# Experts after a linear attention: weight parts loaded earlier, two row transposes placed later

## The chip, the cores and the metric

The kernel runs on one NeuronCore of one Trainium2 chip. The metric is device time in microseconds (us) of one execution, as the median of several runs. The profile shows one execution, with every instruction's start and duration by engine: PE (TensorE, with PEld for its weight loads), DVE (VectorE), ACT (ScalarE), POOL (GpSimd), SP (SyncE, which here only issues DMA transfers).

## The reference, cut to what matters

The change lies in the last of three stages, a mixture of eight experts in which each token goes to its two best experts. x is the stage's input of 2304 rows by 512.

```python
top2 = np.argpartition(-noisy_logits, 2, axis=1)[:, :2]
...
for e in range(E):
    for k in range(2):
        mask = top2[:, k] == e
        ...
        h = np.maximum(x[mask] @ w1[e], 0.0)
        out[mask] += top2_w[mask, k, None] * (h @ w2[e])
```

w1[e] is 512 by 1024, w2[e] is 1024 by 512. The other two stages (attention with exponential features, a wide layer with a maximum of three products) are not touched.

## The kernel before, in words

Every float32 product is made of three matmuls, since each operand is split into a rounded high part and the remainder: high by high, high by low, low by high. So each weight part is held as a pair `wh`, `wl`, and each activation as a pair too (`gx`, and `hh`, `hl` for the hidden layer).

**Units.** The experts' work is a list of units, numbered n. Unit 0 is expert 0 with 512 rows, unit 1 is expert 0 again with 128 rows, and units 2 to 8 are experts 1 to 7 with 608 rows each (row tiles 0 to 4: four of 128 rows and one of 96). In units 2 to 8 the first product is done in a scheme with seven block products instead of eight (`product`, L1213): in two rounds of two column blocks f, each round goes through the seven products in the order 1, 6, 7, 4, 5, 3, 2. Their sums are formed by DVE (`sum7`, L1232, tiles `u`, `v`, `t`), ACT takes the maximum with zero and makes `hh` (L1241, L1242), and POOL or DVE makes `hl` (L1251, L1249). A product's PSUM bank is free for a later product when ACT or DVE has read it. The banks are three named `s`, three named `p` and `k`, and two named `t`, each used in turn. Then `expert2` (L1354) multiplies the hidden layer by w2: 24 matmuls for each row tile, into a `p` or `k` bank. In the second round the two banks of product 4 are `t` banks, and the first two transposes of the next unit's rows use them next.

**Rows of the next unit.** POOL gathers the token rows of the next unit by indirect DMA (`gather_x`, L1139) into one of two buffers (`gx`, `xg` in the trace). PE transposes a row tile in four small matmuls (`turn_x`, L1149; `turns7` in the plan). Then ACT and DVE split the transposed rows and form block sums (`x_quarters`, `x_sums`; `rows7(j)` for a pair of row tiles). Row tile i + 2 is gathered into the buffer that row tile i leaves. Results go out by a gather of the old rows (`pv`), a DVE multiply-add (`o`, L1362) and a scatter (`out_dram`, L1364), all in POOL's queue.

**Weight parts.** A part of 128 by 1024 comes in three steps: a 512 KB transfer into one of two `raw` buffers, issued by SP (L1381 for w2, L1387 for w1); the copy to `wh` on ACT (L1434); the remainder `wl` on DVE (L1442). So the transfer of part n + 2 waits for the `wl` of part n. The sums of w1 blocks that products 6, 7, 5 and 3 need were made ahead of time and come ready split from memory (`wh<-sums`, `wl<-sums`, L1437), each waiting until PE has done with the part whose place it takes.

**Order.** All instructions of PE, ACT, DVE and SP are written out by a plan: each step is given a time on a rough clock (`clock[0]`, advanced by `pe` with the length of a PE step), and the steps are sorted by it. The times set only the order in each engine's queue. Queues run strictly in order, so a waiting instruction holds up those behind it. POOL's indirect transfers keep the order of the plan too. `refill_at(i, t, lead)` puts the transfer of part i at t - lead, its `wh` at t and its `wl` at t + 1.2, counted from the clock at which it is called.

For the refill behind unit 1, six parts are loaded. This text calls them A to F in the order of their transfers: A is the w1 part for product 2 of unit 2; B, C, D and E are the four w2 parts of unit 2, in the order in which `expert2` uses them; F is the w1 part for product 1 of unit 3. They are x = 0, 1, 3, 4, 2, 5 in the code. Behind them come G and H, the w1 parts for products 4 and 2 of unit 3.

Of the kernel before, what the change touches and what calls it, by code (L numbers as in the profile page):

```python
# [38 lines left out]
def tile_linear_attention__then__moe__then__noisy_top2_moe(  # L39
# [29 lines left out]
    F2 = FF2 // P  # L69
# [53 lines left out]
    def bank_acc():  # L123
        turns["acc"] += 1
        return bank_k() if turns["acc"] % 3 == 0 else bank_p()
# [973 lines left out]
    def sizes(M):  # L1099
        return [min(P, M - i * P) for i in range((M + P - 1) // P)]  # L1100
# [96 lines left out]
    def seven(n):  # L1197
        return isinstance(n, int) and n > SEVEN
# [139 lines left out]
    def expert2(n, e, M, i, fs=tuple(range(F2))):  # L1338
        m = sizes(M)[i]
        cs = slice(i * P, i * P + m)  # L1340
        p_ = st.pop(("eo", n, i)) if fs[0] else bank_acc()[:m]
        if seven(n):
            fs = (0, 1, 4, 5, 6, 7, 2, 3)
        for f in fs:
            wh, wl = WE[e, (len(ORDER7) if seven(n) else KD) + f // 2]
            hh, hl = st["eh", n, f]
            fw = slice((f % 2) * DM, (f % 2) * DM + DM)
            if seven(n):
                ps_ = slice((i // 2) * 2 * P + i % 2, (i // 2 + 1) * 2 * P, 2)
                hh, hl = (h[:, ps_] if i < 4 else h[:, cs] for h in (hh, hl))  # L1350
            else:
                hh, hl = (h[:, cs] for h in (hh, hl))
            for r, (a, b_) in enumerate(((hh, wh), (hh, wl), (hl, wh))):
                nc.tensor.matmul(p_, a, b_[:, fw], start=(f == 0 and r == 0),  # L1354
                                 stop=(f == (3 if seven(n) else F2 - 1) and r == 2))
        st["eo", n, i] = p_
# [182 lines left out]
    def pe(dur, f, *x):  # L1539
        at(clock[0], f, *x)  # L1540
        clock[0] += dur
# [44 lines left out]
    for i, n in enumerate(late_ones[1:]):  # L1586
        t = END + (3.2 + 2.6 * i + 3.0 * (i > 5) if i else 0.2)
# [143 lines left out]
    for n, (e, M, row0) in enumerate(units):  # L1731
        n_now[0] = n
        nsp = 1 if M <= 512 else 2
        cw = M // nsp
        nxt = n + 1 < len(units)
        if nxt:
            e2, M2, row2 = units[n + 1]
            nt2 = len(sizes(M2))
        g0 = clock[0]
        d1 = 3 * KD * cw / 2400  # L1740
        if seven(n):
            for two in ((0, 1), (2, 3)):
                for q_ in ORDER7:
                    for f in two:
                        pe(2 * 3 * HN / 2400, product, n, e, q_, f)
                        d0, d = (-0.03, 0.01) if two[0] and q_ == ORDER7[-1] else (0.02, 0.44)
                        after(d0, sum7, n, q_, f)
                        if q_ in PART7:
                            after(d0 + d, relu7, n, q_, f)
                            after(d0 + 2 * d, low7, n, q_, f)  # L1750
                    if two[0]:
                        room(base(e) + ORDER7.index(q_))
        elif M > P:
            for f in range(F2):
                for s in range(nsp):
                    if n == 0:
                        for i in range(2):
                            pe(d1 / 2, expert1, n, e, M, f, s, cw, range(2 * i, 2 * i + 2))
                            if f < 2:
                                tail(NCHUNK - 1, 2 * f + i)  # L1760
                    else:
                        pe(d1, expert1, n, e, M, f, s, cw)
                    after(0.0, expert_hidden, n, f, s, cw)
                if n == 0 and f == 1:
                    after(0.0, open_experts)
                    tp = clock[0] + 0.01
        else:
            pe(2.56, tile1, n, e, 0)
            after(0.0, tile_relu, n, 0)
            pe(1.28, tile1, n, e, 1, range(2))  # L1770
            pe(0.45, tile_turn, n, 0)
            after(0.0, tile_hidden, n, 0)
            pe(1.28, tile1, n, e, 1, range(2, KD))
            after(0.0, tile_relu, n, 1)
            after(0.01, gather_prev, 1, 0, cap_b, 0)
        if seven(n):

            own = [i for i in range(base(e), base(e) + len(ORDER7))
                   if i < len(pairs) and not summed(*pairs[i])]
            for i, t in zip(own, (7.0, 9.5, 16.5)):  # L1780
                refill_at(i, t, 9.0)
        elif n:
            rooms(base(e), 2)
            for i in range(2):
                after(0.3 + 0.6 * i, w2_high, *pairs[base(e) + i])
        if n == 4:
            st["table"] = overflow_table()
        if n in (4, 5):
            for i in range(9 - (n == 5)):
                at(g0 + 2.0 + 2.3 * i, next, st["table"])  # L1790

        if n > 1:
            tp = g0 + 12.0
        if n != 1:
            for i in range(min(3, len(sizes(M)))):
                at(tp, gather_prev, n, e, M, i)
        if n == 0:
            for n_ in (1, 2):
                _, M_, row_ = units[n_]
                at(tp + 17.0, load_meta, n_, row_, M_, 0)  # L1800
            at(tp + 17.1, gather_x, 1, cap_b, 0, N + 1)
            at(tp + 20.0, gather_x, 2, cap, 0, N + 1)
        elif n > 1 and nxt:
            for i in range(2):
                at(g0 - 3.0, gather_x, n + 1, M2, i, N + 1)
        if 0 < n and n + 2 < len(units):
            at(g0 + (6.2 if n == 1 else 2.3), load_meta, n + 2, units[n + 2][2], cap, 0)
        d2 = 3 * F2 * DM / 2400
        def turns7(i, n=n):
            pe(0.45, turn_x, n + 1, cap, i)  # L1810
            if i + 2 < len(sizes(cap)):
                after(0.02, gather_x, n + 1, cap, i + 2, N + 1)

        def rows7(j, wait=1.6):
            after(0.5, x_quarters, j)
            after(wait, x_sums, j)

        if M <= P:
            pe(0.7 * 2, expert2, n, e, M, 0, range(2))
            pe(0.45, tile_turn, n, 1)  # L1820
            after(0.0, tile_hidden, n, 1)
            turns7(4)
            rows7(2)
            pe(0.7 * 2, expert2, n, e, M, 0, range(2, 4))
            pe(d2 / 2, expert2, n, e, M, 0, range(4, F2))
            after(0.0, expert_out, n, e, M, 0)
        else:
            if nxt and n > 0:
                for i in range(2):
                    turns7(i)  # L1830
                rows7(0)
            if not nxt:
                after(0.9, settle)
            for i in range(len(sizes(M))):
                if n == 0 and i == 2:
                    pe(0.45, turn_x, 1, cap_b, 0)
                    after(0.02, gather_x, 2, cap, 1, N + 1)
                    turns7(0, 1)
                if n == 0 and i == 3:
                    turns7(1, 1)  # L1840
                    rows7(0)
                pe(d2, expert2, n, e, M, i)
                if n == 0:
                    after((-0.01, -0.01, 0.5, 0.5)[i], expert_out, n, e, M, i)
                else:
                    after(0.95 if nxt and i == 1 else -0.01, expert_out, n, e, M, i)
                if n == 0 and i == 2:
                    after(0.51, gather_prev, n, e, M, 3)
                elif n and i + 3 < len(sizes(M)):
                    after(0.96 if nxt and i == 1 else 0.0, gather_prev, n, e, M, i + 3)  # L1850
                if nxt and n > 1:
                    if i == 1:
                        turns7(2)
                        turns7(3)
                        rows7(1)
                    if i == 3:
                        turns7(4)
                        rows7(2)
        if n == 0:
            turns7(2, 1)  # L1860
            turns7(3, 1)
            rows7(1, 2.6)
        if n:
            if seven(n):
                i = base(e) + len(ORDER7)
                rooms(i, 4)
                for x, t in enumerate((0.4, 3.8, 12.7, 15.8)):
                    refill_at(i + x, t, 9.0)
            else:
                i = base(e) + 2  # L1870
                rooms(i, 6)
                for x, t in zip((0, 1, 3, 4, 2, 5), (0.4, 3.4, 6.2, 12.7, 15.8, 18.6)):
                    refill_at(i + x, t, 4.0 if x == 5 else 9.0)

    ET = mybir.EngineType
# [56 lines left out]
```

## Time and profile before

| what | value |
|---|---|
| median of 3 runs | 935.04 us (933.77 to 935.37) |
| profiled execution | 935.69 us |
| its span from first to last instruction | 934.1 us |
| outside the span | 1.6 us |
| PE busy | 924.6 us, 99% of the span |
| DVE, POOL, ACT busy | 616.9, 540.7, 491.6 us |
| granted PE clock | 0.998 of full speed (2.4 GHz) |
| moved by DMA | 178.07 MB, mean 191 GB/s |

The PE is busy nearly all the time. Durations of matmuls overlap (they are pipelined), so progress of PE is read from the distance between starts. A wait is read in the bracket behind an instruction: the idle time before it, and what ended it.

### The profile page before, as it was taken

To read this page: it belongs to the slowest core of one execution; us is meant where nothing else is said; L and a number is where in the kernel's file an instruction comes from. 1 tells how busy PE (TensorE), PEld (TensorE's weight loads), DVE (VectorE), ACT (ScalarE), POOL (GpSimd) and SP (SyncE) were. 2 spreads that over 40 slices of the span, in tenths; PEclk is the share of its full clock that TensorE was granted. 3 is DMA by queue.
4 is the path that set the end of the run, shared out by engine and by line. 5 is a ranking of instruction groups with operands and counts; after the bars stand their busy time and mean duration, and the time that the engine had idled before them with its cause. 6 is when DMAs were issued, how large, how long until landed. Compare 5 with 4: busy or idle time off the path is not lost. (4 is left out here: it accounts for less than half of the span.)

```text
span 934.1 us, 18533 instructions
## 1 busy us (share of the span) xinstructions
PE 924.6 (99%) x6817; PEld 805.1 (86%) x6817; DVE 616.9 (66%) x1292; ACT 491.6 (53%) x1056; POOL 540.7 (58%) x598
## 2 busy tenths in 40 slices
PE   9999999999999999999999999999999999999997
PEld 7677777799999999999997889798898989898895
DVE  6999999997563737364564367667576767567641
ACT  7999999554333334343445147355463635455340
POOL 6788898645554645646443546465574746455362
PEclk9999999999999999999999999999999999999999
DMA  7676663544757575857575367666575856748212
GB/s 195 171 220 170 185 192 104 193 154 138 227 178 251 181 239 178 248 170 216 164 218 204 91 224 248 242 215 233 174 254 175 285 166 204 264 155 296 94 34 73
DMA packets 131101, 178.07 MB, mean 191 GB/s; under 512 B 35998, under 2 KB 90398, under 8 KB 131010
## 3 DMA queue, kind: packets, MB, share of 16 engines
q1 hardware_dynamic: 119522, 146.94, 49.5%
q0 software_dynamic: 10928, 29.62, 9.5%
q8 instruction: 54, 0.88, 0.4%
q10 hardware_dynamic: 560, 0.33, 0.1%
q14 instruction: 37, 0.30, 0.1%
HBM read 123.05 MB, written 51.24 MB: 187 GB/s over the span
## 5 line engine op out<-in xcount | busy, mean ns | idle before, releaser
L899 PE MATMUL s<-xh,wh 128*128 128x384 f32 x432 | 147.3, 341 | 0.0
L899 PE MATMUL s<-xh,wl 128*128 128x384 f32 x432 | 145.2, 336 | 0.0
L899 PE MATMUL s<-xl,wh 128*128 128x384 f32 x432 | 145.1, 336 | 0.0
L1364 POOL DMA_INDIRECT out_dram<-o,emeta x40 | 47.7, 1191 | 97.6 <-DVE o L1362 30.1
L909 DVE TENSOR_TENSOR a<-s,a 128x384 f32<-128x384 f32 x72 | 40.0, 555 | 88.4 <-PE s L899 87.3
L899 PEld LDWEIGHTS s<-xh,wh 128*128 128x128 f32 x432 | 81.1, 188 | 5.4 <-DVE a L909 2.5
L1354 PE MATMUL p<-wh,hh 128*128 128x512 f32 (+1 forms) x208 | 82.9, 399 | 0.0
L1354 PE MATMUL p<-wh,hl 128*128 128x512 f32 (+1 forms) x208 | 82.5, 396 | 0.2 <-POOL hl L1251 0.2
L899 PEld LDWEIGHTS s<-xl,wh 128*128 128x128 f32 x432 | 81.1, 188 | 1.4
L1354 PE MATMUL p<-wl,hh 128*128 128x512 f32 (+1 forms) x208 | 82.1, 395 | 0.0
L899 PEld LDWEIGHTS s<-xh,wl 128*128 128x128 f32 x432 | 81.1, 188 | 0.0
L1442 DVE TENSOR_TENSOR wl<-raw,wh 128x1024 fp32r<-128x1024 f32 x57 | 69.3, 1221 | 14.8 <-ACT wh L1434 13.8
L1213 PE MATMUL s<-gx,wh 128*128 128x304 f32 x336 | 72.5, 302 | 0.0
L1410 POOL TENSOR_TENSOR raw<-raw 128x256 f32<-128x256 f32 x28 | 24.5, 876 | 74.9 <-DMA raw<-in_moe_w_dram 63.4
L132 DVE TENSOR_TENSOR gx<-t,gx 128x512 fp32r<-128x512 f32 (+3 forms) x88 | 41.0, 480 | 35.7 <-ACT gx L131 32.8
L1434 ACT ACTIVATE wh<-raw 128x1024 fp32r<-128x1024 f32 x57 | 58.9, 1053 | 9.4 <-DMA raw<-in_moe_w_dram 9.4
L245 POOL TENSOR_TENSOR nm<-nm,bits 128x512 int32<-128x512 int32 (+1 forms) x32 | 38.2, 1205 | 40.9 <-DVE nm L235 16.1
L916 ACT ACTIVATE hh<-a 128x384 fp32r<-128x384 f32 x36 | 18.8, 523 | 81.1 <-DVE a L909 76.9
L131 ACT ACTIVATE gx<-t 128x512 fp32r<-128x512 f32 (+3 forms) x88 | 36.5, 437 | 39.3 <-DVE t L1188 30.5
L1213 PEld LDWEIGHTS s<-gx,wh 128*128 128x128 f32 x336 | 55.6, 189 | 0.7
L1077 POOL DMA_INDIRECT meta<-mt,si x36 | 38.8, 1077 | 29.7 <-DVE si L1073 20.5
L1213 PE MATMUL s<-gx,wl 128*128 128x304 f32 x168 | 50.9, 303 | 0.0
(323 smaller groups left out, 2635.0 us busy)
## 6 DMA issues: line engine op xcount, KB each, us to landing
raw<-in_moe_w_dram SPq DMA_DIRECT2D x57, 512.0 KB
raw<-in_moe_w_dram SPq DMA_DIRECT2D x56, 256.0 KB
sums<-qh SPq DMA_DIRECT2D x28, 512.0 KB
sums<-raw SPq DMA_DIRECT2D x28, 512.0 KB
wh<-sums SPq DMA_DIRECT2D x28, 512.0 KB
wl<-sums SPq DMA_DIRECT2D x28, 512.0 KB
bits<-in_moe_w_dram SPq DMA_DIRECT2D x18, 512.0 KB
out_dram<-zrow SPq DMA_DIRECT2D x9, 512.0 KB
```

The costliest lines, as they stand in the source:

```text
L131: nc.scalar.activation(hi, src, AF.Copy)
L132: nc.vector.tensor_tensor(lo, src, hi.bitcast(F32), op=ALU.subtract)
L245: in_order(nc.gpsimd.tensor_tensor(m_[:, i:i + w], m_[:, i:i + w], low[:, i:i + w], op=ALU.add))
L899: nc.tensor.matmul(p_, a[:, d, fs], b_, start=(n == 0), stop=(n == 3 * KD - 1))
L909: nc.vector.tensor_tensor(a, p_, st.pop("a"), op=ALU.max)
L1077: ins = nc.gpsimd.indirect_dma_start(out=meta, out_offset=bass.IndirectOffsetOnAxis(ap=si[:, t, kk:kk + 1], axis=0), in_=mt[:, t, kk, :], ...
L1213: nc.tensor.matmul(bk["p"], a[:, d, fs], b_[:, d, :], start=(d == 0 and i == 0), stop=(d == 1 and i == 2))
L1354: nc.tensor.matmul(p_, a, b_[:, fw], start=(f == 0 and r == 0), stop=(f == (3 if seven(n) else F2 - 1) and r == 2))
L1364: alone(e, nc.gpsimd.indirect_dma_start(out=out, out_offset=bass.IndirectOffsetOnAxis(ap=mt[:m, i, 1:2], axis=0), in_=o[:m], in_offset=Non ...
L1410: ins = nc.gpsimd.tensor_tensor(a22, a21, a22, op=ALU.add)
L1434: nc.scalar.activation(WE[e, i][0], st["w2", e, i], AF.Copy)
L1442: nc.vector.tensor_tensor(wl, st.pop(("w2", e, i)), wh.bitcast(F32), op=ALU.subtract)
```

## The change

In the refill behind unit 1, the times of the `wh` copies of A to F were 0.4, 3.4, 6.2, 12.7, 15.8 and 18.6 us on the plan's clock, and are now 0.4, 1.8, 4.8, 7.6, 10.4 and 13.2. Their transfers, which are placed 9 us ahead (4 for F), move with them. In unit 2 only, the transposes of row tiles 2 and 3 of unit 3 stood behind row tile 1 of `expert2`; they stand now in the middle of row tile 2, between its matmuls for four column blocks and for the other four. For this `expert2` takes a range of blocks, and translates it to its own order of blocks.

```diff
         if seven(n):
-            fs = (0, 1, 4, 5, 6, 7, 2, 3)
+            fs = [(0, 1, 4, 5, 6, 7, 2, 3)[f] for f in fs]
...
-                pe(d2, expert2, n, e, M, i)
+                if n == 2 and i == 2:
+                    pe(d2 / 2, expert2, n, e, M, i, range(4))
+                    turns7(2)
+                    turns7(3)
+                    rows7(1)
+                    pe(d2 / 2, expert2, n, e, M, i, range(4, F2))
+                else:
+                    pe(d2, expert2, n, e, M, i)
...
-                    if i == 1:
+                    if i == 1 and n > 2:
                         turns7(2)
...
-                for x, t in zip((0, 1, 3, 4, 2, 5), (0.4, 3.4, 6.2, 12.7, 15.8, 18.6)):
+                for x, t in zip((0, 1, 3, 4, 2, 5), (0.4, 1.8, 4.8, 7.6, 10.4, 13.2)):
                     refill_at(i + x, t, 4.0 if x == 5 else 9.0)
```

What this does to the queues is shown at three places. The first is SP's queue from part A on. Before, the row with x3 ends with A, the next L1381 is B, the x3 behind it are C, D and E, and the lone L1387 is F:

```order
L1387 DMA raw<-in_moe_w_dram 128x2x512 x3
L1437 DMA wh<-sums 128x1024
L1437 DMA wl<-sums 128x1024
L1381 DMA raw<-in_moe_w_dram 128x2x512
L1437 DMA wh<-sums 128x1024
L1437 DMA wl<-sums 128x1024
L1381 DMA raw<-in_moe_w_dram 128x2x512 x3
L1437 DMA wh<-sums 128x1024
L1437 DMA wl<-sums 128x1024
L1387 DMA raw<-in_moe_w_dram 128x2x512
```

The same place in the changed kernel:

```order
L1387 DMA raw<-in_moe_w_dram 128x2x512 x3
L1381 DMA raw<-in_moe_w_dram 128x2x512
L1437 DMA wh<-sums 128x1024
L1437 DMA wl<-sums 128x1024
L1437 DMA wh<-sums 128x1024
L1437 DMA wl<-sums 128x1024
L1381 DMA raw<-in_moe_w_dram 128x2x512 x3
L1387 DMA raw<-in_moe_w_dram 128x2x512
L1437 DMA wh<-sums 128x1024
L1437 DMA wl<-sums 128x1024
```

B stands now ahead of the two sums for unit 2, and F ahead of the first sum for unit 3. The three other sums for unit 3, and G and H behind them, keep their places.

The second place is DVE's queue at the start of unit 2's seven products. Before (the L1442 rows are the `wl` of A, B and C; `u`, `v`, `t` are the sums of the first round):

```order
L1442 TENSOR_TENSOR wl<-raw,wh 128x1024
L1232 TENSOR_TENSOR u<-s_7245,t 128x304
L1232 TENSOR_TENSOR u<-k,t 128x304
L1232 TENSOR_TENSOR v<-s_7269,u 128x304
L1232 TENSOR_TENSOR v<-p_7279,u 128x304
L1442 TENSOR_TENSOR wl<-raw,wh 128x1024
L1232 TENSOR_TENSOR t_7288<-t_7288,v 128x304
L1232 TENSOR_TENSOR t_7300<-t_7300,v 128x304
L1249 SCALAR_TENSOR_TENSOR hl_7223<-t_7288,hh_7222 128x304
L1232 TENSOR_TENSOR v<-s_7309,v 128x304
L1232 TENSOR_TENSOR u<-s_7309,u 128x304
L1249 SCALAR_TENSOR_TENSOR hl_7235<-t_7300,hh_7234 128x304
```

And in the changed kernel:

```order
L1442 TENSOR_TENSOR wl<-raw,wh 128x1024
L1232 TENSOR_TENSOR u<-s_7245,t 128x304
L1442 TENSOR_TENSOR wl<-raw,wh 128x1024
L1232 TENSOR_TENSOR u<-k,t 128x304
L1232 TENSOR_TENSOR v<-s_7273,u 128x304
L1232 TENSOR_TENSOR v<-p_7282,u 128x304
L1232 TENSOR_TENSOR t_7291<-t_7291,v 128x304
L1442 TENSOR_TENSOR wl<-raw,wh 128x1024
L1232 TENSOR_TENSOR t_7301<-t_7301,v 128x304
L1249 SCALAR_TENSOR_TENSOR hl_7223<-t_7291,hh_7222 128x304
L1232 TENSOR_TENSOR v<-s_7313,v 128x304
L1232 TENSOR_TENSOR u<-s_7313,u 128x304
```

The `wl` of B moved ahead of three sums, and that of C ahead of three sums and two `hl`. Further on, D, E and F move the same way: D stands behind the first of product 3's two sums, E directly ahead of the second round's first sum, F behind that round's two `u`. ACT's `wh` copies move with them: C's follows B's directly, D's stands behind the first `v` pair of round one, E's ahead of the last `t` pair of round one, and F's behind the two copies of product 1 of round two.

The third place is PE's queue between row tiles 1 and 2 of unit 2 (`t` rows are the transposes, `k` is the bank of row tile 1, `p` that of row tile 2). Before:

```order
L1354 MATMUL k<-wh,hl_7396 128x512
L1149 MATMUL t_7673<-exact,gx 128x128 x4
L1149 MATMUL t_7678<-exact,xg 128x128 x4
L1354 MATMUL p_7684<-wh,hh_7220 128x512
L1354 MATMUL p_7684<-wl,hh_7220 128x512
```

And in the changed kernel, twelve matmuls of row tile 2 further on:

```order
L1354 MATMUL p_7673<-wl,hh_7234 128x512
L1354 MATMUL p_7673<-wh,hl_7235 128x512
L1149 MATMUL t_7694<-exact,gx 128x128 x4
L1149 MATMUL t_7699<-exact,xg 128x128 x4
L1354 MATMUL p_7673<-wh,hh_7387 128x512
```

In POOL's queue one row moves with them: the gather of row tile 4 goes from ahead of the scatter of row tile 1 to behind the `pv` gather of row tile 4. No instruction is added or taken away on any engine.

## Rows read from the trace of the kernel before

**Rows 1.** The page, part 1: busy us, share of the span, instructions.

```profile
PE 924.6 (99%) x6817; PEld 805.1 (86%) x6817; DVE 616.9 (66%) x1292; ACT 491.6 (53%) x1056; POOL 540.7 (58%) x598
```

**Rows 2.** The waits of PE in the whole span: us in total, times, longest.

```profile
PE t L1149 <- DMA gx<-x2d,emeta: 0.9, 1, 0.9
...
PE p L1354 <- POOL hl L1251: 0.2, 1, 0.2
```

**Rows 3.** The timeline of PE in unit 2, around its two waits.

```profile
583.41 0.39 PE L1354 MATMUL p<-wl,hh 128*128 128x512 f32 x1
583.95 0.51 PE L1354 MATMUL p<-wh,hl 128*128 128x512 f32 x1 [0.16 <-POOL hl L1251]
...
590.25 0.40 PE L1354 MATMUL k<-wl,hh 128*128 128x512 f32 x1
590.48 0.40 PE L1354 MATMUL k<-wh,hl 128*128 128x512 f32 x1
591.76 0.50 PE L1149 MATMUL t<-exact,gx 128*128 128x128 f32 x4 [0.89 <-DMA gx<-x2d,emeta]
...
592.76 0.48 PE L1354 MATMUL p<-wh,hh 128*128 128x512 f32 x1
```

**Rows 4.** The timeline of PE at the same pair of transposes without a wait, between units 0 and 1.

```profile
541.40 0.39 PE L1354 MATMUL p<-wh,hl 128*128 128x512 f32 x1
...
542.27 0.46 PE L1286 MATMUL s<-wh,x 128*128 128x512 f32 x1
```

**Rows 5.** The timeline of SP: transfers of C to E, of F, of G and H.

```profile
556.79 8.91 SPq L1381 DMA_DIRECT2D raw<-in_moe_w_dram  x3
...
573.69 0.38 SPq L1387 DMA_DIRECT2D raw<-in_moe_w_dram  x1
...
577.58 3.58 SPq L1387 DMA_DIRECT2D raw<-in_moe_w_dram  x2
```

**Rows 6.** The timeline of POOL in unit 2: an hl, the last hl pair, a gather.

```profile
580.20 1.26 POOL L1251 TENSOR_TENSOR hl<-v,hh 128x304 fp32r<-128x304 f32 x1 [0.92 <-ACT hh L1242]
...
583.05 1.67 POOL L1251 TENSOR_TENSOR hl<-t,hh 128x304 fp32r<-128x304 f32 x2
584.86 0.98 POOL L1139 DMA_INDIRECT gx<-x2d,emeta  x1
```

**Rows 7.** DMA from 586 to 590 us: busy tenths of 16 engines in 40 slices.

```profile
DMA  9999999998999999999999999898996979989889
```

**Rows 8.** The timeline of ACT: wh of B and C, last hh, wh of G and H.

```profile
556.84 1.05 ACT L1434 ACTIVATE wh<-raw 128x1024 fp32r<-128x1024 f32 x1
...
562.23 1.05 ACT L1434 ACTIVATE wh<-raw 128x1024 fp32r<-128x1024 f32 x1
...
583.03 0.48 ACT L1242 ACTIVATE hh<-t 128x304 fp32r<-128x304 f32 x1
...
588.96 1.06 ACT L1434 ACTIVATE wh<-raw 128x1024 fp32r<-128x1024 f32 x1 [1.28 <-DMA raw<-in_moe_w_dram]
591.87 1.06 ACT L1434 ACTIVATE wh<-raw 128x1024 fp32r<-128x1024 f32 x1 [1.85 <-DMA raw<-in_moe_w_dram]
```

**Rows 9.** DMA from 560 to 565 us: busy tenths of 16 engines in 40 slices.

```profile
DMA  9966664210000000000099700066969999997511
```

**Rows 10.** The timeline of DVE in unit 2: first u, wl of B, an hl, wl of F.

```profile
557.42 0.47 DVE L1232 TENSOR_TENSOR u<-s,t 128x304 f32<-128x304 f32 x1 [0.66 <-ACT t L1227]
...
560.26 1.22 DVE L1442 TENSOR_TENSOR wl<-raw,wh 128x1024 fp32r<-128x1024 f32 x1
...
577.62 0.47 DVE L1249 SCALAR_TENSOR_TENSOR hl<-t,hh 128x304 fp32r<-128x304 f32 x1
...
579.53 1.21 DVE L1442 TENSOR_TENSOR wl<-raw,wh 128x1024 fp32r<-128x1024 f32 x1
```

**Rows 11.** The timeline of PE: second round's product 2, and the transposes of row tile 1.

```profile
576.50 0.44 PE L1213 MATMUL s<-gx,wh 128*128 128x304 f32 x2
...
578.48 0.51 PE L1149 MATMUL t<-exact,xg 128*128 128x128 f32 x4
```

## Prediction

> **What bounds the kernel now.** I read the page first: PE is busy 924.6 of 934.1 us [rows 1]. So a change that adds and removes no work can give back only what PE waits. The second view is therefore the list of PE's waits. In the experts it holds two, both in unit 2, both once: 0.9 us for a gather of rows, 0.2 us for a low part made by POOL [rows 2]. The third is PE's timeline there, since a wait costs more than its bracket says. Matmuls of `expert2` start 0.23 us apart (590.25, 590.48). From the last one of row tile 1 to the first one of row tile 2, over eight transposes, it is 592.76 - 590.48 = 2.28 us [rows 3]; over the same eight without a wait it is 542.27 - 541.40 = 0.87 [rows 4]. The gather costs 1.41 us. At 583.41 the step is 0.54 instead of 0.23: the low part costs 0.31 [rows 3]. The most that can be won is about 1.7 us, 0.18%.
>
> **Why the gather is late.** POOL issues it at 584.86, right behind its last `hl` pair [rows 6]. Part F, for which a raw buffer came free late, was issued at 573.69; behind it in SP's queue six sums, then G and H, the last of them about 581 [rows 5]. That is nine transfers of 512 KB in 7.5 us, and the 16 DMA engines are at nine tenths or more through nearly all of 586 to 590 [rows 7]. G, issued at 577.58, holds ACT until 588.96, 11.4 us; H until 591.87, and the gather ends PE's wait at 591.76, within 0.1 us of H [rows 8, 3]. The gather is the tail of a pile of weight transfers.
>
> **Part one: A to F earlier.** I work the new order forward with the durations of the rows: `wh` 1.05, `wl` 1.22, a sum 0.47 with the next 0.39 behind it.
> B: its transfer no longer waits behind two sums; it was never late, so nothing follows from that alone. Its `wh` ends at 556.84 + 1.05 = 557.9, the first `u` at the same moment, so `wl` runs to 559.1, where it ran to 561.5 [rows 8, 10]. D can be issued 2.4 us earlier.
> C: issued at 556.79 as before [rows 5]. Its landing shows nowhere as a wait. It is not after 562.23, when its `wh` began unheld [rows 8]; the traffic dies away at about 561.2, ten slices of 0.125 us after 560 [rows 9]. I take 561.1, a transfer of 4.3 us. Then `wh` to 562.2, `wl` to 563.4; E goes then instead of at 565.3 (556.79 + 8.91, less the 0.38 of one issue).
> D lands near 563.4; its `wh` stands behind the first `v` pair, which C has pushed back, and its `wl` ends near 567.8. F is issued then: 5.9 us earlier than 573.69.
> E's `wl` ends near 572.3. F lands near 572; its `wh` waits for ACT's two copies of product 1 and ends at 574.2, its `wl` at 575.5, where it ended at 580.7 [rows 10].
> G and H need the buffers of E and F and stand behind sums that wait for PE to finish product 5 (about 575.0). They go at 575.5 to 576 instead of 577.58 and 580.8, and F and the first sums are out of the pile. By 585 the pile should be gone.
>
> Where this can hold PE: three sums and then four others now stand behind a `wl`. Round one has slack. In round two, product 2 starts at 576.50 [rows 11] in the bank of a `v` sum that now ends near 575.9: 0.6 us spare. The transposes of row tile 1, at 578.48 [rows 11], need the bank of product 4 after DVE's second `hl`, which ended at 577.62 + 0.47 = 578.1 [rows 10]. Now F's `wl` runs 574.3 to 575.5 ahead of four sums, the first `hl` (held by ACT to 577.2), two sums and this `hl`: it ends near 578.8. PE is held 0.4 us, a new wait. The bounds are 0 (parts landing 0.5 us sooner) and 1.0.
> It costs less than it shows. POOL's `hl` chain ends row tile 0: last `hh` 583.03, POOL done at 583.05 + 1.67 = 584.7 [rows 8, 6]. F's `wl` used to stand ahead of DVE's last two sums at 579.53; now it does not, which makes up for the late start. I get the last `hh` at 583.2 and POOL done at 584.6. So PE, held 0.4 us at the start, waits less at the `hl`, and row tile 0 ends when it did: 0.0, between -0.3 and +0.5.
>
> There is a rule that speaks against this. The `hl` at 580.20 took 1.26 us, beside F's `wl` (579.53 to 580.74), against 0.84 for each of the pair at 583.05 [rows 6, 10]. The Trainium skill (SBUF — State Buffer, Who interferes with whom) says that DVE and GpSimd share a port pair under an exclusive lock, so that one blocks the other for a whole instruction; the row agrees, though 0.42 us is less than the 0.54 of the overlap. By that rule the last `hl` of round one is now caught by E's `wl`, some 0.35 us, which goes on to F and to the hold at row tile 1; the sum would be -1.1 instead of -1.4.
>
> **Part two: the transposes twelve matmuls later.** They would start at 590.75 without a wait; twelve matmuls at 0.23 later is 593.5. Even where part one brought nothing, the gather is there at 591.76. The wait goes, by either part: -1.41, at worst -1.0 if one buffer's data still lags. Splitting `expert2` adds no instruction; eight transposes cost 0.87 between matmuls wherever they stand. What is late next: the split of these rows on ACT and DVE ends about 1.5 us later than it did, and has a row tile and a half, 8.4 us, until the transposes of row tile 4 need the banks. The gather of row tile 4 in POOL's queue goes behind a scatter and a `pv` gather, some 4 us later, and has the same 8 us. I cost both at nothing; without that cover they would cost what they are late.
>
> **Sum.** -1.41 + 0.0 = -1.4 us: the profiled execution 935.69 to 934.3. It lies 0.65 above the median of the runs, so for the median 935.04 - 1.4 = **933.6**.
>
> **Rivals.**
> *C lands late, and the kernel is slower.* C's `wh` and `wl` now stand ahead of all that ACT and DVE do for round one after the first sums, and D, E and F follow from it. Past 561.1, each us that C is late moves F's `wl` and with it PE's hold by one us. At 562.5 the gain is used up, at 564.4 the kernel is 0.2% slower. For it: G took 11.4 us in the pile. Against: C goes at the same moment beside the same traffic, and was there by 562.23. Halfway between 4.3 and 11.4 us, it would land 3.6 late: 935.04 + 3.6 - 1.4 = 937.2.
> *The holds eat the gain.* The hold at row tile 1 is 1.0, and POOL's chain starts late by as much, or the gather, sharing queues with G and H as they now come, still lags: 934.8 to 935.2. For it: DVE's start of round two is tight to 0.6 us in two places. Against: PE and POOL each absorb part of it.
> *All of it is won.* C, D and F land half a us sooner, there is no hold and the 0.31 goes too: 935.04 - 1.72 = 933.3.
>
> **How the numbers follow.** Forecast 0.62, holds 0.17, all won 0.14, slower 0.07. A measurement of this kernel tells about 0.2%, 1.87 us, from no change; no case here gains that much. But the three runs lie 1.6 us apart, so a median may stand 0.5 off (an estimate from that spread): 0.15 of the forecast's chance and 0.09 of the third rival's fall beyond 933.17, together 0.24 for faster. Slower has 0.06 of the first rival and 0.01 of the holds, and 0.69 is left for within 0.2%. The range leaves out a tenth on each side: from 932.6 (all won, 0.7 of scatter) to 935.4 (the holds, 0.4 of scatter); the slower rival lies outside.
>
> **What the next profile would show.** Right: no wait for `gx` in PE's list; the transposes of row tiles 2 and 3 unheld, near 593.5; F issued before 569 and H before 577; G's and H's `wh` without a wait; POOL's last `hl` done by 585; a wait of up to 0.5 us at the transposes of row tile 1. Part one is wrong if H still goes after 579 or if DVE's sums of round one end more than 2 us later than they did. The prediction fails if PE's first matmul of unit 3 comes less than 1.0 or more than 1.9 us sooner, or if a wait appears in another unit, where I expect no change.

## The result

| | median | runs |
|---|---|---|
| before | 934.97 us (933.77 to 935.49) | 6 |
| changed | 939.37 us (937.84 to 940.63) | 6 |

The ratio is 1.0052, with a 95% interval of 1.0042 to 1.0062: slower by 4.4 us, where 933.6 was forecast. The profiled execution of the changed kernel took 939.75 us, its span is 938.2 [before: 934.1]. Its page and PE's waits:

```profile
PE 925.9 (99%) x6817; PEld 806.8 (86%) x6817; DVE 615.6 (66%) x1292; ACT 491.7 (52%) x1056; POOL 541.0 (58%) x598
...
PE t L1149 <- DMA gx<-x2d,emeta: 3.4, 2, 3.0
...
PE t L1149 <- DVE hl L1249: 0.3, 1, 0.3
...
PE p L1354 <- DVE u L1232: 0.2, 1, 0.2
```

The two waits of [rows 2] are gone, and others stand there (us in total, times, longest). One of them, for a gather, has 3.0 of the lost us. Two of the places in PE's timeline before, which no row above shows:

```profile
529.41 0.46 PE L1149 MATMUL t<-exact,xg 128*128 128x128 f32 x4
529.71 0.51 PE L1149 MATMUL t<-exact,gx 128*128 128x128 f32 x4
...
578.18 0.47 PE L1149 MATMUL t<-exact,gx 128*128 128x128 f32 x4
...
578.90 0.51 PE L1354 MATMUL p<-wh,hh 128*128 128x512 f32 x1
```

And PE's timeline of the changed kernel:

```profile
529.41 0.46 PE L1149 MATMUL t<-exact,xg 128*128 128x128 f32 x4
530.26 0.50 PE L1149 MATMUL t<-exact,gx 128*128 128x128 f32 x4 [0.40 <-DMA gx<-x2d,emeta]
...
578.79 0.46 PE L1149 MATMUL t<-exact,gx 128*128 128x128 f32 x4
579.59 0.53 PE L1149 MATMUL t<-exact,xg 128*128 128x128 f32 x4 [0.34 <-DVE hl L1249]
580.35 0.51 PE L1354 MATMUL p<-wh,hh 128*128 128x512 f32 x1 [0.23 <-DVE u L1232]
...
594.10 0.39 PE L1354 MATMUL p<-wh,hl 128*128 128x512 f32 x1
594.34 0.46 PE L1149 MATMUL t<-exact,gx 128*128 128x128 f32 x4
...
594.97 0.47 PE L1354 MATMUL p<-wh,hh 128*128 128x512 f32 x1
...
603.23 0.40 PE L1354 MATMUL p<-wh,hl 128*128 128x512 f32 x1
606.66 0.70 PE L1149 MATMUL t<-exact,gx 96*128 96x96 f32 x4 [3.04 <-DMA gx<-x2d,emeta]
607.16 0.72 PE L1354 MATMUL k<-wh,hh 128*96 128x512 f32 x1
607.68 0.63 PE L1354 MATMUL k<-wl,hh 128*96 128x512 f32 x1
...
610.13 0.39 PE L1354 MATMUL k<-wl,hh 128*96 128x512 f32 x1
```

Read by starts, from the top:

- At 529.6, ahead of unit 1, two transposes stand 0.85 apart instead of 0.30: 0.55 lost.
- At row tile 1's transposes, first to `expert2`, 1.56 pass (578.79 to 580.35), where the kernel before took 0.72 (578.18 to 578.90): 0.84 lost.
- Between row tile 2's halves the eight transposes take 0.87, as in [rows 4], so the 1.41 of [rows 3] is won, and with it the 0.31 of the low part.
- At row tile 4 the transposes begin 3.43 after the last matmul instead of 0.23: 3.20 lost.
- Behind them the matmuls stand 0.42 to 0.52 apart. From the transposes to the eighth matmul it is 3.47 (606.66 to 610.13); in an experiment below where PE waited 1.1 us (e7) it is 2.02: 1.45 lost.

The sum is 0.55 + 0.84 - 1.41 - 0.31 + 3.20 + 1.45 = 4.3, against 4.1 between the two spans.

The view by windows of the changed kernel shows what the last 1.45 are: PE's clock, granted at 1.00 until the wait ends, then at 0.50, which is 1.2 GHz.

```profile
core 0: us, PE busy (x) PEld busy (x) DVE busy (x) ACT busy (x) POOL busy (x), PEclk, DMA share, GB/s
603.50:606.60 3.10, 0.12 (x1) 0.00 (x0) 0.75 (x1) 0.00 (x0) 1.99 (x2) 1.00 0.83 309
606.60:609.80 3.20, 3.14 (x10) 2.29 (x11) 1.28 (x5) 0.87 (x4) 1.87 (x3) 0.50 0.38 105
```

The Trainium skill (TensorE: Matmul & The Clock Gate, What's actually happening) has the array at 1.2 GHz after it has been idle and at 2.4 after it has been busy; this trace agrees: 0.50 is granted behind 3.0 us of standing, although the standing itself is still shown at 1.00.

Why the gather came late is read in POOL's timeline. First the kernel before, with the gather of row tile 4 at 592.99:

```profile
591.63 1.06 POOL L1329 DMA_INDIRECT pv<-out_dram,ic  x1 [0.28 <-POOL ic L1326]
592.99 0.94 POOL L1139 DMA_INDIRECT gx<-x2d,emeta  x1 [0.30 <-PE t L1149]
596.75 1.01 POOL L1364 DMA_INDIRECT out_dram<-o,emeta  x1 [2.82 <-DVE t L1188]
```

Then the changed kernel, with the same gather in the last row:

```profile
592.48 1.06 POOL L1329 DMA_INDIRECT pv<-out_dram,ic  x1 [0.28 <-POOL ic L1326]
598.78 1.01 POOL L1364 DMA_INDIRECT out_dram<-o,emeta  x1 [5.24 <-DVE b L1188]
599.85 0.22 POOL L1326 TENSOR_SCALAR ic<-emeta 96x1 int32<-96x1 int32 x1
600.35 1.00 POOL L1329 DMA_INDIRECT pv<-out_dram,ic  x1 [0.28 <-POOL ic L1326]
601.66 1.20 POOL L1139 DMA_INDIRECT gx<-x2d,emeta  x1 [0.31 <-issue]
```

DVE's timeline has the data of that scatter, and SP's a weight part that goes 0.41 us behind the gather:

```profile
592.04 0.75 DVE L1362 SCALAR_TENSOR_TENSOR o<-k,emeta,pv 128x512 f32<-128x512 f32 x1
...
602.07 0.37 SPq L1381 DMA_DIRECT2D raw<-in_moe_w_dram  x1
```

The gather of row tile 4 goes at 601.66 instead of 592.99, 8.7 us later. It stands behind the scatter of row tile 1, and that scatter waits. The bracket names DVE, but DVE's `o` for this row tile ran from 592.04 to 592.79, long before, so something else ended the wait. In the code the scatter of an expert must wait for the `pv` gathers issued ahead of it (`alone`: they read what it writes), here that of row tile 3. The experiments test this.

### The profile page after: what moved, and what is told of

Its sections match the earlier page's. It is cut to its first block, busy times and chain, and to the rows that moved or that the text cites. A ratio compares the mean times of both kernels' runs of the same rounds, so it can differ in the third digit from the quotient of the medians.

```text
span 938.2 us, 18535 instructions
## 1 busy us (share of the span) xinstructions
PE 925.9 (99%) x6817; PEld 806.8 (86%) x6817; DVE 615.6 (66%) x1292; ACT 491.7 (52%) x1056; POOL 541.0 (58%) x598
## 5 line engine op out<-in xcount | busy, mean ns | idle before, releaser
L1442 DVE TENSOR_TENSOR wl<-raw,wh 128x1024 fp32r<-128x1024 f32 x57 | 69.1, 1220 | 15.8 <-ACT wh L1434 14.8
```

Source lines behind the costliest of these rows:

```text
L1442: nc.vector.tensor_tensor(wl, st.pop(("w2", e, i)), wh.bitcast(F32), op=ALU.subtract)
```

## The experiments

After the result, three theories: *queue* (the gather behind the scatter in POOL's queue), *refill* (the early weight parts), *place* (transposes in the middle of a row tile). Ratios are to the kernel before, run on the same chip; a median is of eleven executions, e8's of five. Times within a run are of its one profiled execution.

**e1_refill_alone**: the times of part one alone, on the kernel before.

> Part one alone: the six weight parts at their new times, the transposes of row tiles two and three where they were. Three theories. Queue: the loss is POOL's queue, where the gather of row tile 4 now stands behind the scatter of row tile 1, which itself waits for the pv gather of row tile 3; part one has no share in that. Then this run has what part one does by itself: 0.56 lost at 529.6, 0.9 lost at the transposes of row tile 1 of unit 2, 1.95 won in row tiles 0 and 2: -0.5 against the kernel before, 934.5, and no wait for gx at row tile 4. Refill: the early weight parts themselves hold the row tiles and make the gathers late: +4 against before, about 939. Place: the transposes in the middle of a row tile are what costs: 934.5, as the first.

Measured 934.44 us, ratio 0.9997 (0.9988 to 1.0006), and PE's list has no wait for `gx`: refill falls.

**e2_turns_alone**: part two alone.

```diff
-                for x, t in zip((0, 1, 3, 4, 2, 5), (0.4, 1.8, 4.8, 7.6, 10.4, 13.2)):
+                for x, t in zip((0, 1, 3, 4, 2, 5), (0.4, 3.4, 6.2, 12.7, 15.8, 18.6)):
```

> Part two alone: the transposes in the middle of row tile two (the third), the six weight parts at their old times. Queue: the wait at row tile 2 goes (-1.41). The scatter of row tile 1 is released when its pv gather has landed, 596.75 as before; the gather of row tile 4 behind it is issued near 599.6, lands 4.9 later at 604.5, and PE, which comes there at 604.1 - 1.4 = 602.7, waits 1.8, and then runs up to 1.5 longer at half clock: +0.4 to +1.9, so 935.4 to 936.9. Refill: nothing is left of the loss and the wait at row tile 2 is gone: -1.4, 933.6. Place: the loss is all here, +4 or more, 939.

Measured 933.89 us, ratio 0.9992 (0.9983 to 1.0001): neither part is slower by itself, and the queue theory's 935.4 to 936.9 missed. Place falls, and the queue theory by itself does too, as it was put. POOL's timeline of this run:

```profile
590.72 1.06 POOL L1329 DMA_INDIRECT pv<-out_dram,ic  x1 [0.28 <-POOL ic L1326]
595.59 1.01 POOL L1364 DMA_INDIRECT out_dram<-o,emeta  x1 [3.81 <-DVE gx L132]
...
598.47 0.93 POOL L1139 DMA_INDIRECT gx<-x2d,emeta  x1 [0.31 <-issue]
```

And PE's, at the transposes of row tile 4:

```profile
601.54 0.39 PE L1354 MATMUL p<-wh,hl 128*128 128x512 f32 x1
601.78 0.44 PE L1149 MATMUL t<-exact,gx 96*128 96x96 f32 x4
```

The order is that of the changed kernel, and the gather is late here too, but it goes 3.31 us ahead of PE's need and is there in time. In the changed kernel PE's need is at 603.46 (603.23 + 0.23), 1.80 after the issue. So part two spent nearly all of the slack, and with part one 1.5 more is gone: the scatter goes 6.30 behind the `pv` gather instead of 4.87. And the gather itself takes 5.00 there, issue to transposes, instead of at most 3.31. The weight part issued at 602.07 stands at the same place in e2, 1.4 ahead of PE's need (600.37); the gather, going later, has come up to it.

**e3_gather_first**: the changed kernel, with the scatter of row tile 1 and what follows it put behind the gather.

```diff
-                    after(0.95 if nxt and i == 1 else -0.01, expert_out, n, e, M, i)
+                    after((3.06 if n == 2 else 0.95) if nxt and i == 1 else -0.01, expert_out, n, e, M, i)
...
-                    after(0.96 if nxt and i == 1 else 0.0, gather_prev, n, e, M, i + 3)
+                    after((3.07 if n == 2 else 0.96) if nxt and i == 1 else 0.0, gather_prev, n, e, M, i + 3)
```

(and a dependency in `expert_out` that keeps this scatter behind the gather on POOL).

> The changed kernel, with the gather of row tile 4 back ahead of the scatter of row tile 1 in POOL's queue; nothing else is moved on any other engine. Queue: the 3.2 us wait at the transposes of row tile 4 and the 1.5 us of slow matmuls behind it are gone: -4.7 against the changed kernel, 934.7, -0.5 against the one before. Refill or place: the wait goes elsewhere or stays, 938 to 939.

Measured 934.17 us, ratio 0.9994 (0.9985 to 1.0003): by the two ratios 0.58% less than the changed kernel, 5.4 us, with no wait at row tile 4. So the gather's place in POOL's queue is necessary for the loss.

**e4_turns_gather_first**: the same edit with the old times of A to F.

> Part two alone, with the gather of row tile 4 ahead of the scatter of row tile 1 in POOL's queue, and the weight parts at their old times. Queue: only the wait at row tile 2 is gone, -1.4 against the kernel before: 933.6, with the 0.3 at the low part of POOL still there and no wait at row tile 4. Refill: the same 933.6. Place: slower than before by some us, 938.

Measured 933.79 us, ratio 0.9989 (0.9980 to 0.9998), with no wait at row tile 4.

**e5_gather_between**: only the second line of e3's diff, so that the gather goes behind the scatter, and ahead of `ic` and `pv`.

> The changed kernel, with the gather of row tile 4 between the scatter of row tile 1 and the pv gather of row tile 4: still behind the scatter, but ahead of two POOL instructions. After the first four runs the theory is a chain: the scatter of row tile 1 waits for the pv gather of row tile 3; the gather of row tile 4 is issued 2.9 us behind that scatter; alone it takes 3.0 us (part two alone, issued 598.47, transposes at 601.8 unheld), and 4.9 where a 512 KB weight part is issued 0.4 behind it (the changed kernel). Here it goes 1.8 earlier and 2 us ahead of the weight part, so it lands near 603 to 604.8; PE needs it at 603.5: a wait of 0 to 1.5, 934.5 to 937. Rival (traffic: the gather is late because of the weight transfers, wherever it stands in the queue): the wait stays over 2.5, 938 to 939.

Measured 934.26 us, ratio 0.9999 (0.9990 to 1.0008), just under the expected 934.5 to 937: no wait at row tile 4. Two POOL instructions fewer ahead of it are enough.

**e6_busy_wait**: 13 matmuls whose product nobody reads, ahead of row tile 4's transposes (`filler`, a new function, issues them).

```diff
                     if i == 3:
+                        if n == 2:
+                            pe(0.0, filler, n, e, 3, 13)
                         turns7(4)
```

> The changed kernel with 13 matmuls more, whose product nobody reads, ahead of the transposes of row tile 4: PE works through most of the 3.0 us for which it waited. The slow matmuls behind the wait (0.43 apart instead of 0.23, seven of them, granted clock 0.50) are the second half of the loss. If they come from PE's standing idle, they go: -1.5 against the changed kernel, 937.9, though the gather lands no sooner. If they come from something else (the traffic, the operands), the time stays at 939.4 or rises a little.

Measured 936.96 us, ratio 1.0026 (1.0017 to 1.0035). PE's timeline of this run, from the 13 matmuls on:

```profile
602.48 3.18 PE L1363 MATMUL k<-wh,hh 128*128 128x512 f32 x13
605.76 0.50 PE L1149 MATMUL t<-exact,gx 96*128 96x96 f32 x4
...
606.38 0.39 PE L1354 MATMUL k<-wl,hh 128*96 128x512 f32 x1
606.61 0.40 PE L1354 MATMUL k<-wh,hl 128*96 128x512 f32 x1
```

From where PE would have come to the transposes it is 3.28 (602.48 to 605.76), against 3.20 in the changed kernel (603.46 to 606.66): the filled wait is no shorter. But the matmuls behind it stand 0.23 apart, and the granted clock is 1.00:

```profile
605.70:608.90 3.20, 3.14 (x16) 2.36 (x17) 1.45 (x6) 0.87 (x4) 1.99 (x2) 1.00 0.41 119
```

So the slow stretch came from PE's standing. The kernel gained 2.4 where 1.5 was expected. Between the two profiled executions 0.9 of that is there before the transposes (605.76, 606.66), and not from the filler: this execution was 1.04 ahead at 528.37 already, ahead of e6's edit, and lost nothing at 529.6, where the changed one lost 0.55. Whether the median's excess is such scatter is not shown.

**e7_third_later**: the `wl` behind which the 512 KB transfer at 602.07 waits, put behind row tile 3's `o`.

```diff
-            for i, t in zip(own, (7.0, 9.5, 16.5)):
+            for i, t in zip(own, (7.0, 9.5, 21.5 if n == 2 else 16.5)):
```

> The changed kernel, with the low part of the third weight part of unit 3 behind the o of row tile 3 on DVE, so that the 512 KB transfer that waits for its raw buffer goes near 605.6 instead of 602.07, after the gather of row tile 4 instead of 0.4 us behind its issue. Chain: the gather takes 3.0 to 3.5 us instead of 4.9, and lands near 605: the wait at row tile 4 falls from 3.0 to 1.1-1.6, 936 to 937.5. Rival (the gather takes 4.9 by itself, the neighbour does nothing): 939.4.

Measured 935.81 us, ratio 1.0011 (1.0001 to 1.0020), just under the expected 936 to 937.5. The transfer goes at 605.54, and POOL's timeline has the gather here:

```profile
601.50 0.93 POOL L1139 DMA_INDIRECT gx<-x2d,emeta  x1 [0.31 <-issue]
```

PE's timeline of the same run, around the wait:

```profile
603.20 0.39 PE L1354 MATMUL p<-wh,hl 128*128 128x512 f32 x1
604.69 0.49 PE L1149 MATMUL t<-exact,gx 96*128 96x96 f32 x4 [1.10 <-DMA gx<-x2d,emeta]
...
606.71 0.39 PE L1354 MATMUL k<-wl,hh 128*96 128x512 f32 x1
```

The gather went at nearly the same time as in the changed kernel (601.50, 601.66), and from issue to transposes it took 3.19 instead of 5.00. So the weight part issued 0.4 us behind it cost 1.8. After this wait of 1.1 us the granted clock stayed at 1.00:

```profile
604.70:608.00 3.30, 3.30 (x17) 2.47 (x18) 2.43 (x7) 0.87 (x4) 2.45 (x3) 1.00 0.58 122
```

**e8_h_later**: the `wl` of H put back behind row tile 1's `o` (9.5 to 12.0 in the same line).

> The changed kernel, with the low part of H behind the o of row tile 1 on DVE, as it stood before, so that the two 512 KB transfers that wait for the buffers of G and H don't go 1.1 us apart just ahead of the pv gather of row tile 3. If these two are what made that pv gather take 5.5 us (4.1 with part two alone), it takes 4.1 to 4.5, the scatter is released 1.0 to 1.4 sooner and the gather of row tile 4 with it: the wait falls to about 1.8, 937 to 938.5. If they are not, 939.4.

Measured 939.86 us, ratio 1.0057 (1.0043 to 1.0070): missed. The two transfers are apart now (589.39 and 592.05), but the `pv` gather goes at 590.84 between them, its issue takes 2.11 us, and the scatter follows it 7.74 later instead of sooner. That spacing the two out would mend it was wrong, and what makes this `pv` gather longer with part one stays open: in e2 the two go 0.32 ahead of it and 1.79 behind, in e8 1.45 ahead and 1.21 behind, and to the scatter it is 4.87 and 7.74. In the four traces with part one and this stretch of POOL's queue (the changed kernel, e5, e6, e7) it is 6.30 to 6.37; that it is shorter without part one rests on e2's one trace, and e4, without part one but with the gather in between, has 6.00.

**e9_pv_behind**: the changed kernel, with the `pv` gather of row tile 3 behind the scatter of row tile 1.

```diff
-                    after(0.96 if nxt and i == 1 else 0.0, gather_prev, n, e, M, i + 3)
+                    after(0.96 if nxt and i == 1 else d2 + 0.955 if n == 2 and i == 0 else 0.0, gather_prev, n, e, M, i + 3)
```

> The changed kernel, with the pv gather of row tile 3 moved behind the scatter of row tile 1 in POOL's queue. The gather of row tile 4 stays behind the scatter and now has three more instructions between. Theory: what held the queue is the scatter's wait for that pv gather to land (5.5 us); without it the scatter goes at 592.9, when o is there, the two pv gathers at about 594.4 and 595.9, the gather of row tile 4 near 597.2, 4.4 sooner than in the changed kernel; it lands by 600.5 to 602, before PE comes at 603.5: no wait, 934.5. Rival (the place in the queue costs by itself, through the instructions ahead): the gather goes no sooner than 601.7 and the time stays at 939.

Measured 934.35 us, ratio 0.9998 (0.9989 to 1.0007). POOL's timeline of this run:

```profile
592.67 1.00 POOL L1364 DMA_INDIRECT out_dram<-o,emeta  x1 [1.18 <-DVE o L1362]
...
594.24 1.07 POOL L1329 DMA_INDIRECT pv<-out_dram,ic  x1 [0.28 <-POOL ic L1326]
...
595.86 1.01 POOL L1329 DMA_INDIRECT pv<-out_dram,ic  x1 [0.27 <-POOL ic L1326]
597.17 0.93 POOL L1139 DMA_INDIRECT gx<-x2d,emeta  x1 [0.31 <-issue]
```

This shows the mechanism. The gather has more ahead of it than in the changed kernel and goes 4.5 us sooner, because the scatter no longer waits for a `pv` gather, only for `o`, which its bracket now names.

**e10_b_back**: e3 with B's time at 3.4.

> As e3_gather_first, with B's time back at 3.4 and the other five parts early. B's transfer then no longer goes at 521.2 beside the loads of emeta. The gather behind those loads should wait 0.8 to 1.2 us for them, as in the two kernels without B there, instead of 2.0 to 2.2, as in the three with it; the transposes at 529.6 lose nothing, where they lost 0, 0.6 and 1.2 in those three. Against e3_gather_first (934.2): 0 to -1.2, so about 933.5. Rival (chance in the scatter of meta, B has no share): the gather still waits 2 us, 934.2.

Measured 934.44 us, ratio 0.9997 (0.9988 to 1.0006): no better than e3. The gather behind the `emeta` loads waited 1.29 here, as expected, but 2.27 in the next kernel, whose B is late too. Whether B cost the 0.55 at 529.6 stays open: of the eight traces with B early, two lose something there (0.55 in the changed kernel, 1.05 in e3), of the five with B late none does.

**e11_f_late**: e10 with F's time at 17.2.

> As e10_b_back, with F's split back behind the first sums of round two (time 17.2 instead of 13.2); C, D and E stay early, the gather of row tile 4 stays ahead of the scatter. If F's low part ahead of DVE's sums is what holds PE at the transposes of row tile 1 (0.6 to 0.9 more there with part one), the hold goes: 0.7 less than e10_b_back, near 933.0. Rival: H, which needs F's buffer, goes late again, and the hl wait of row tile 0 (0.3) or the gather wait (1.4) is back: 933.6 to 934.6.

Measured 933.91 us, ratio 0.9992 (0.9983 to 1.0001). PE's timeline of this run at row tile 1's transposes:

```profile
577.45 0.47 PE L1151 MATMUL t<-exact,gx 128*128 128x128 f32 x4
577.75 0.51 PE L1151 MATMUL t<-exact,xg 128*128 128x128 f32 x4
```

0.30 apart, unheld; in e10 they stand 1.12 apart (577.82, 578.94). So F's early `wl` is what holds PE there. But a wait for POOL's `hl` is back (0.2 in PE's list), and the time is the rival's, 933.6 to 934.6. The intervals of e10 and e11 overlap. Of the versions run, e4, with part two alone and the gather kept ahead of the scatter, is the only one whose whole interval lies below the kernel before, by 0.02% to 0.2%.

## Why the prediction was wrong

**The step that failed** is "The gather of row tile 4 in POOL's queue goes behind a scatter and a `pv` gather, some 4 us later, and has the same 8 us. I cost both at nothing". It counted the instructions that the gather is moved past and not what the first of them waits for. The trace of before had it: its scatter went at 596.75 after an idle of 2.82, so a gather behind it and behind `ic` and `pv` goes 2.9 later, near 599.6, 6.7 us later and not 4. Of "the same 8 us" e2 had 3.31 left and the changed kernel 1.80, and the gather needed 3.19 (e7) to 5.00. So part two by itself just fits (e2). With part one the scatter goes 6.30 behind the `pv` gather instead of 4.87, the gather goes later still and meets a weight part, and 3.20 + 1.45 are lost. That the scatter's wait is for the `pv` gather is shown by e9, the gather's place by e3, the weight part's 1.8 by e7, the clock by e6. That the loss needs part one too is shown by e2, whose longest execution (935.16) is shorter than the changed kernel's shortest (937.84). That part one acts by a longer `pv` gather rests on e2's one trace, and why it would stays open. "without that cover they would cost what they are late" left out the clock, the 1.45.

**Part one.** Its timings came out: F was issued at 568.48 and G and H at 576.36 and 576.88, 0.4 to 0.9 later than worked out, of which 0.55 is from 529.6; their `wh` ran without a wait; the second `hl` ended at 579.53. The hold was in the right place and mis-sized: 0.84 instead of 0.4, 0.50 of it at the transposes and 0.34 because a sum `u` behind that `hl` held the first matmul too. Its size is also not fixed: in the nine traces with F early it is 0.27 (e5) to 1.16 (e7, e10), in e2, e4 and e11, with F late, nothing. "row tile 0 ends when it did: 0.0, between -0.3 and +0.5" is +0.5 (0.84 - 0.31), at its bound.

The catch of an `hl` on POOL by E's `wl`, which the prediction put at 0.35 and left out of its sum, came and was 0.17: the last `hl` of round one, at 572.57, took 1.03, beside that `wl` (571.66 to 572.89), against 0.86 for the one before it. ACT waited for it, and F's `wh` stood behind.

**B.** "it was never late, so nothing follows from that alone" looked only at who needs B. Its transfer now goes at 521.24, beside the loads of `emeta`. The gather behind them was late, and 0.55 was lost at 529.6 in this execution, a wait in another unit, which the prediction had named as a sign of its failing. B's share in it is open.

**Part two's gain.** 1.41 came as predicted, and the 0.31 on top, which the forecast had set against the hold.

**The rivals.** None was this one. *C lands late* had the sign, and half the size with its price of 2.2 us, but by another mechanism that did not occur: the `wh` of C and all behind it came when worked out. The two parts alone add up to -0.0011 in the ratio (e1, e2) and together give +0.0052: the loss is in their meeting, and the two were costed one by one.

## What to carry to other kernels

When an instruction moves in an in-order queue, read the idle time ahead of each instruction that it now stands behind, and ask what really ends it. Here a scatter that must follow a gather of the same memory held the queue until that gather was done, 4.9 to 7.7 us from issue to issue, and a bracket that names an engine which was long done hid it. When two edits each use up slack of the same transfer, cost them together. And ask what the clock adds to a wait of PE: 1.45 us behind 3.0 here, nothing behind 1.1.

## What was not expected of the hardware

After waits of 3.0 and 3.7 us (the changed kernel, e8) PE's granted clock fell to 0.50 once it worked again, and after a wait of 1.1 (e7) it did not. In the changed kernel it was low from the end of the wait; in e8 the matmuls get slow only 1.1 us after PE had resumed, as PE's timeline of e8 shows:

```profile
605.69 0.49 PE L1149 MATMUL t<-exact,gx 96*128 96x96 f32 x4 [3.69 <-DMA gx<-x2d,emeta]
...
606.77 0.57 PE L1354 MATMUL k<-wh,hh 128*96 128x512 f32 x1
607.13 0.63 PE L1354 MATMUL k<-wl,hh 128*96 128x512 f32 x1
```

The window behind these rows has the clock, at 0.50:

```profile
607.00:609.50 2.50, 2.50 (x7) 1.63 (x6) 1.72 (x7) 0.68 (x3) 1.99 (x2) 0.50 0.55 210
```

A gather of 96 rows took 3.2 us from issue to use with no 512 KB transfer issued beside it (e7), at most 3.3 with one issued 1.9 us behind it (e2), 3.6 with one 1.6 us ahead of it (e8), and 5.0 with one 0.4 us behind it (the changed kernel), while POOL was still issuing the gather (1.20 us instead of 0.93): a transfer issued later can slow one begun before it.
